# A fused attention and feed-forward kernel: the dilated heads' v loads issued from ScalarE's queue

## Chip, cores and metric

One NeuronCore of a Trainium2 chip runs the whole kernel. The metric is device time of one execution in microseconds (us); lower is better.

## What is computed

Attention over q, k and v of shape (4 batches, 8 heads, 576 positions, 64), then two feed-forward layers on the 2304 x 512 result. All in float32; the weights come as float64.

```
mask_plain = (rel >= 0) & (rel < window)                                   # heads 0 to 3, window 32
mask_dil = (rel >= 0) & (rel < window * dilation) & (rel % dilation == 0)  # heads 4 to 7, dilation 4
scores = where(mask, scale * q @ k.T, -1e9)
attn = exp(scores - max); attn = attn / (sum(attn) + 1e-9)
x = (attn @ v) as [2304 tokens, 512]
x = (silu(x @ w_gate) * (x @ w_val)) @ w_out                               # d_ff 1536
out = (((x @ w1) * (x @ w2)) @ w3) @ w_out2                                # d_ff 1024
```

## The kernel before

**Stages.** Attention runs first, in 18 superblocks of 128 tokens, software-pipelined: step u of the loop (L531, u from -3 to 19) works on several superblocks at once. Then TensorE does the feed-forward layers in 20 slices of 128 hidden units by 5 groups of tokens (L472 up, L565 and L585 down, L612 the product w3 @ w_out2). Each float32 product is three matmuls of high and low parts.

**Loads of attention.** `load_qk(u)` (L292) brings a superblock's q and k into `near` (heads 0 to 3, L297) and `far` (the dilated heads, L302). `load_v(u)` (L305) brings v into `vnear` (L314, two blocks of up to 96 rows) and `vfar` (L319, 96 rows of the dilated heads). A `far` or `vfar` window that crosses a multiple of 144 rows, the length of one dilated stream, is cut into two loads, so the 18 superblocks have 27 `vfar` loads. All of these, and the weights' loads (`raw_w`, L143 and L148), are issued from the SP queue, in the order of the program: it holds no list or planner of its own, and an instruction waits for all before it on its queue. Buffers: three of `near` and of `far`, four of `vnear` and of `vfar`; a load waits until the last reader of its buffer is done.

**One step u** (`attention_step`, L495, then `attention_end`, L522) issues in this order: loads of q and k for superblock u+5; loads of v for u+2; on ScalarE the copies of the transposed probabilities out of PSUM (`t_p_out`, L417, u-1) and of the attention result (`x_out_hi`, L451, u-2); exp on ScalarE (L389, u+1); scores on TensorE (L368, u+2), on VectorE mask and maximum (L377, L383), on GpSimd the subtraction (L384); the transposes of q and k on TensorE (`pnear` L341, `pfar` L348, u+3), with copies on ScalarE (L335, L336 for the 32 keys kept from the superblock before, then L343, L344, L349, L350); a piece of weight conversion on VectorE (L114 to L124); the sums and reciprocals on VectorE (L393 to L396, u+1) and the normalisation on GpSimd (L402); the low part of the attention result on VectorE (L455, u-2). At its end TensorE transposes the probabilities of u (L411) and multiplies those of u-1 with v (`av`, L431).

So the v of superblock u+2, called for in step u, is read at the end of step u+3, and the `vfar` buffer that it takes was last read by av of u-2, at the end of step u-1; `x_out_hi(u-2)` on ScalarE reads the result of that same av.

Of the kernel before, what the change touches and what calls it, by code (L numbers as in the profile page):

```python
# [19 lines left out]
P = 128  # L20
WINDOW = 32
DIL = 4
QB = 64
KW = QB + WINDOW
NIDLE = 8
NEG = -1.0e9
# bounds of a float64's upper word (sign off, read as float32) between which float32 has its exponent
UP_LO = 2.0 ** -15
UP_HI = 2.0 ** 16 * (1.0 + (2 ** 23 - 2 ** 20 - 1) / 2.0 ** 23)

# [2 lines left out]
def attention_ffn_kernel(  # L33
# [14 lines left out]
    nc = tc.nc  # L48
# [10 lines left out]
    RES = S // DIL  # L59
# [12 lines left out]
    wp = ctx.enter_context(tc.tile_pool(name="wp", bufs=1))  # L72
    sp = ctx.enter_context(tc.tile_pool(name="sp", bufs=1))
    ps = ctx.enter_context(tc.tile_pool(name="ps", bufs=1, space=PSUM))
    # tokens in two parts: what attention still writes is apart from what the first groups read
    CUT = groups[(len(groups) + 1) // 2][0]
    spans = ((0, CUT), (CUT, NT))
    x_hi = [xp.tile([P, KT, b - a], F32R, name=f"x_hi{a}") for a, b in spans]
# [3 lines left out]
        i = int(t0 >= CUT)  # L82
        return x[i][:, kk, t0 - spans[i][0]:t0 - spans[i][0] + n]

    # keep the tensor engine busy until the first loads are there: its clock is halved when it comes from idling
    zeros = xp.tile([P, 512], BF16, name="zeros")
    nc.vector.memset(zeros, 0.0)
    idle = ps.tile([P, 512], F32, tag="po3", name="idle", bufs=1)
# [7 lines left out]
        return ps.tile([P, 512], F32, tag=tag, name=name, bufs=bufs)  # L96


    # ---------------------------------------------------------------- weights
    WC = 2 * KT * P + DM  # L100
    PW = KT * P
    NCH = NFT + NF2
# [4 lines left out]
        return w.bitcast(I32)  # L107

    def to_f32(dst, raw):
        """float64 words (low, high) of raw -> float32 bits in dst, one instruction at a time."""  # L110
        w = raw.rearrange("p (n t) -> p n t", t=2)
        up, low = w[:, :, 1], w[:, :, 0]
        b = dst.bitcast(I32)
        nc.vector.tensor_scalar(out=b, in0=up, scalar1=0x7FFFFFFF, scalar2=None, op0=ALU.bitwise_and)  # L114
        yield
        nc.vector.tensor_scalar(out=dst, in0=dst, scalar1=UP_LO, scalar2=UP_HI, op0=ALU.max, op1=ALU.min)
        yield
        nc.vector.tensor_scalar(out=b, in0=b, scalar1=3, scalar2=0x3FFFFFFF,
                                op0=ALU.logical_shift_left, op1=ALU.bitwise_and)
        yield  # L120
        nc.vector.scalar_tensor_tensor(out=b, in0=up, scalar=-0x40000000, in1=b,
                                       op0=ALU.bitwise_and, op1=ALU.bitwise_or)
        yield
        nc.vector.scalar_tensor_tensor(out=b, in0=low, scalar=29, in1=b,  # L124
                                       op0=ALU.logical_shift_right, op1=ALU.bitwise_or)
        yield
# [7 lines left out]
                      wp.tile([P, WC], F32R, tag="wlo", name=f"wlo{c}", bufs=2))  # L134
        return whl[c]

    # a job is one [P, PW] piece of float64 weights, loaded ahead and brought to float32 in order
    def job_load(job):
        kind, a, j = job
        raw = wp.tile([P, 2 * PW], I32, tag="wraw", name=f"raw_{kind}{a}_{j}", bufs=3)  # L140
# [30 lines left out]
    jobs = []  # L171

    def jobs_of(c):
        """Jobs of the steps of slice c: by group."""
        res = [[] for _ in groups]
        if c + 1 < NCH:
            first = 1
            if NFT - 1 <= c:
                f = c + 1 - NFT
                res[0].append(("w3", f, 0))  # L180
                res[1].append(("w3", f, 1))
                first = 2
            for j in range(3 if c + 1 < NFT else 2):
                res[first + j].append(("w", c + 1, j))
        if 1 <= c <= NJ:
            res[4].append(("wo", c - 1, 0))
        return res
# [19 lines left out]
    running = run_jobs()  # L207

    def next_job():
        """The rest of a job."""  # L210
        while not next(running):
            pass

# [1 line left out]
    parts = [0]  # L215

    def part_jobs(u):
        """The early jobs, an instruction or two at a time over the superblocks."""
        n = len(early)
        if u >= -2 and (u + 2) % (NU // n - 2) == 0:  # L220
            load_to(min(n, jpos[0] + 1))
        upto = min(PARTS, max(0, (u - 1) * PARTS // (NU - 5)))
        while parts[0] < upto:
            next(running)
            parts[0] += 1

    # ---------------------------------------------------------------- attention
    att = tc.alloc_tile_pool(name="att", bufs=1, side="right")

    # Superblock u, blocks of QB queries with KW keys each:  # L230
    # - first half of the heads: tokens u*P.. of all batches
    # - second half of the heads: indices u*QB.. of the streams (batch, pair of residues), each of RES
    #   indices
    # index of a stream's first query in a superblock (from the superblock's start)
    starts = {}
    for part in range(NU * QB // RES):
        for u in range(NU):
# [7 lines left out]
    def build_masks():  # L245
        gen = att.tile([P, KW], F32, name="m_gen")
        nc.gpsimd.memset(gen, 0.0)
        for h in range(2):
            g = gen[h * QB:(h + 1) * QB, :]
            # row - col + WINDOW >= 0, and col - row - 1 >= 0  # L250
            nc.gpsimd.affine_select(out=g, in_=g, compare_op=ALU.is_ge, fill=NEG,
                                    base=WINDOW, pattern=[[-1, KW]], channel_multiplier=1)
            nc.gpsimd.affine_select(out=g, in_=g, compare_op=ALU.is_ge, fill=NEG,
                                    base=-1, pattern=[[1, KW]], channel_multiplier=-1)
        for u in range(MPER):
            m = att.tile([P, 2, KW], F32, name=f"mask{u}")
            nc.vector.tensor_copy(out=m, in_=gen.rearrange("p (u c) -> p u c", u=1).to_broadcast([P, 2, KW]))
            for h in range(2):
                g = m[h * QB:(h + 1) * QB]
                if (2 * u + h) % NB == 0:  # L260
                    nc.gpsimd.memset(g[:, 0, 0:WINDOW], NEG)
                if u in starts:
                    d = starts[u]
                    if d <= 0:
                        nc.gpsimd.memset(g[:, 1, 0:WINDOW + d], NEG)
                    else:
                        # rows from d on see none of the keys before d
                        w = g[:, 1, 0:WINDOW + d]
                        nc.gpsimd.affine_select(out=w, in_=w, compare_op=ALU.is_ge, fill=NEG, base=d - 1,
                                                pattern=[[0, WINDOW + d]], channel_multiplier=-1)  # L270
            mask.append(m)

    def runs(a, n, size):
        """Rows a..a+n cut at multiples of size: (row, length, index of the part, offset in it)."""
        done = 0
        while done < n:
            part, off = divmod(a + done, size)
            step = min(n - done, size - off)
            yield done, step, part, off
            done += step  # L280
# [4 lines left out]
    near_in, far_in, v_in = {}, {}, {}  # L285

    def stream(src, part):
        """Rows [RES, HH, 2 * D] of a stream: both residues of an index side by side."""
        b, r = divmod(part, RP)
        return src[b, HH:H].rearrange("h (m r) d -> m h (r d)", r=DIL)[:, :, r * 2 * D:(r + 1) * 2 * D]  # L290

# [13 lines left out]
    def load_v(u):  # L305
# [10 lines left out]
        if z:  # L316
            nc.gpsimd.memset(far[0:z], 0.0)
        for row, cnt, part, m in runs(u * QB - WINDOW + z, KW - z, RES):
            nc.sync.dma_start(out=far[z + row:z + row + cnt], in_=stream(v, part)[m:m + cnt])  # L319
        v_in[u] = near, far  # L320

    qkT = {}

    def t_qk(u):
        """Transposed queries (scaled) and keys: partitions are (head's parity, d), or (residue, d)."""
        qn = att.tile([P, HP, P], F32, tag="qn", name=f"qn{u}", bufs=3)
        qf = att.tile([P, HH, QB], F32, tag="qf", name=f"qf{u}", bufs=3)
        kn = att.tile([P, HP, WINDOW + P], F32, tag="kn", name=f"kn{u}", bufs=3)
# [23 lines left out]

    sc, sm, mx, rs, pt_, pT, avp = {}, {}, {}, {}, {}, {}, {}

    # Row tile rt of the scores, half x of its queries: first half of the heads: head 2p+rt, block x;
    # second half: head 2p+x, residue rt.
    def scores(u, rt):
        t = bank("pa", f"sc{u}_{rt}", 2)[:, :NP * KW].rearrange("q (p c) -> q p c", c=KW)
        qn, qf, kn, kf = qkT[u]
# [73 lines left out]
        avp[u] = t  # L433

    def x_parts(x, u):
        """(columns of x, columns of av's result) of superblock u."""
        t = avp[u]
        yield tokens(x, slice(0, HP), u * P, P), t[:, 0:HP, :]
        t = t[:, HP:NP, :].rearrange("d p (h q) -> d p h q", h=2)
# [9 lines left out]
    def x_out_hi(u):  # L449
        for dst, src in x_parts(x_hi, u):  # L450
            nc.scalar.copy(out=dst, in_=src)  # L451
# [3 lines left out]
            nc.vector.tensor_tensor(out=dst, in0=src, in1=hi.bitcast(F32), op=ALU.subtract)  # L455
        avp.pop(u)

    # ---------------------------------------------------------------- feed-forward, slice of hidden units by slice
    st = {}

    upp = {}
# [27 lines left out]
        nc.gpsimd.tensor_tensor(out=sl[:, :n], in0=pr[:, :n], in1=sh[:, :n].bitcast(F32), op=ALU.subtract)  # L489
        st[c, g] = sh, sl  # L490

    # ---------------------------------------------------------------- attention, software-pipelined
    build_masks()

    def attention_step(u):  # L495
        def live(n):
            return 0 <= n < NU
        if live(u + 5):
            load_qk(u + 5)
        if live(u + 2):  # L500
            load_v(u + 2)
        if live(u - 1):
            t_p_out(u - 1)
        if live(u - 2):
            x_out_hi(u - 2)
        if live(u + 1):
            softmax_e(u + 1)
        if live(u + 2):
# [42 lines left out]
            nc.vector.tensor_tensor(out=dst, in0=src, in1=dst, op=ALU.add)  # L551

    def down1(c, g):
        """y of the first layer: channels on partitions."""
        t0, n = groups[g]
        hi, lo = whl[c]
        sh, sl = st.pop((c, g))
# [12 lines left out]
                nc.gpsimd.tensor_tensor(out=xl, in0=y[:, cc, :], in1=xh.bitcast(F32), op=ALU.subtract)  # L570

    def down2(c, g):
        """Output rows: tokens on partitions."""
        t0, n = groups[g]
        hi, lo = whl[c]
        sh, sl = st.pop((c, g))
# [13 lines left out]
    def down(c, g):  # L590
        (down1 if c < NFT else down2)(c, g)

    # ---------------------------------------------------------------- w3 @ w_out2, a row tile ahead of its slice
    w3T = {}

    def fold_t(f, half):
# [66 lines left out]
```

## Time and profile before

| What | Value |
|---|---|
| Time before, median of 3 runs (lowest to highest) | 906.69 us (905.39 to 908.28) |
| Span of the profiled execution (its own time is not listed apart) | 905.6 us |
| TensorE busy | 885.6 us (98%) |
| VectorE busy | 603.3 us (67%) |
| ScalarE busy | 245.2 us (27%) |
| GpSimd busy | 286.5 us (32%) |
| Loads from the SP queue | 60.90 MB |

The profile is one execution, recorded by the hardware. "Busy" counts an engine's instructions, not its waits or its issues of DMAs; SP does nothing but issue and wait, so it is read from its timeline. PE is TensorE, PEld its weight loads, DVE VectorE, ACT ScalarE, POOL GpSimd; an engine's name with a q is its queue. The shares are means over two stages that differ: attention, about the first 103 us, and the feed-forward layers after it. A load has two times: how long its queue took to issue it, and how long from its issue to its landing.

### The profile page before, as it was taken

The numbers are of one execution on the slowest core, as the hardware profiler recorded it, in microseconds if no ns is written. First come the engines' busy times: TensorE is split into PE (matmuls) and PEld (weight loads), VectorE is DVE, ScalarE is ACT, GpSimd is POOL, SyncE is SP. The second block draws the span as 40 slices with busy tenths as digits, with TensorE's granted clock in tenths as the row PEclk, the third lists the DMA queues.
The fourth block names the chain that finished last, engine by engine and source line by source line (L and its number), as shares of the span: only waits on it lengthen the run. The fifth ranks groups of instructions, "written<-read, shape, count | busy, mean of one in ns | idle before, by whom it ended". The sixth has DMA issues, their size and how long they took to land.

```text
span 905.6 us, 13322 instructions
## 1 busy us (share of the span) xinstructions
PE 885.6 (98%) x5256; PEld 744.7 (82%) x5256; DVE 603.3 (67%) x1070; ACT 245.2 (27%) x510; POOL 286.5 (32%) x280
## 2 busy tenths in 40 slices
PE   7898999999999999999999999999999999999998
PEld 4777888888888888888888888888888888888886
DVE  6789755767567676676674687857575747575724
ACT  5777621222122222122212133212121212121211
POOL 6566612323233232232322257321221212121211
PEclk9999999999999999999999999999999999999999
DMA  6896601122112121121210211112020211120014
GB/s 164 187 193 155 171 25 47 47 70 70 48 47 71 47 70 46 47 70 47 70 47 26 67 47 47 47 47 67 27 70 25 70 46 48 47 66 28 1 47 163
DMA packets 79118, 61.75 MB, mean 68 GB/s; under 512 B 35664, under 2 KB 72144, under 8 KB 79056
## 3 DMA queue, kind: packets, MB, share of 16 engines
q1 hardware_dynamic: 79056, 60.90, 23.8%
q8 instruction: 42, 0.69, 0.3%
q14 instruction: 20, 0.16, 0.1%
HBM read 56.16 MB, written 4.72 MB: 67 GB/s over the span
## 4 chain that ended last, share of the span: by engine, by line
PE 90%; DMA 4%; DVE 3%; SPq 1%; ACT 1%; issue 0%; POOL 0%; DVEq 0%; POOLq 0%
PE pa L472 27%; PE pb L472 26%; PE po L565 15%; PE po L585 10%; PE fold L612 5%; DMA far<-in_k_dram 4%; PE av L431 2%; PE pp L411 1%; PE pfar L348 1%; PE sc L368 1%; SPq L302 1%; PE pw L600 1%; DVE o L551 0%; PE pnear L341 0%; ACT x_hi L569 0%
## 5 line engine op out<-in xcount | busy, mean ns | idle before, releaser
L489 POOL TENSOR_TENSOR sl<-pr,sh 128x512 fp32r<-128x512 f32 (+1 forms) x100 | 118.2, 1182 | 332.9 <-ACT sh L488 332.9
L485 DVE TENSOR_TENSOR pr<-pb,ga 128x512 f32<-128x512 f32 (+1 forms) x100 | 63.8, 638 | 223.2 <-PE pb L472 147.5
L472 PE MATMUL pa<-x_hi,whi 128*128 128x512 f32 (+1 forms) x400 | 149.0, 372 | 0.0
L472 PE MATMUL pa<-x_hi,wlo 128*128 128x512 f32 (+1 forms) x400 | 147.6, 369 | 0.0
L472 PE MATMUL pa<-x_lo,whi 128*128 128x512 f32 (+1 forms) x400 | 147.5, 369 | 0.0
L472 PE MATMUL pb<-x_hi,wlo 128*128 128x512 f32 (+1 forms) x400 | 147.1, 368 | 0.0
L472 PE MATMUL pb<-x_hi,whi 128*128 128x512 f32 (+1 forms) x400 | 147.1, 368 | 0.0
L472 PE MATMUL pb<-x_lo,whi 128*128 128x512 f32 (+1 forms) x400 | 147.1, 368 | 0.0
L169 POOL TENSOR_TENSOR wlo<-val_w,whi 128x512 fp32r<-128x512 f32 x52 | 67.0, 1289 | 206.9 <-ACT whi L168 206.8
L551 DVE TENSOR_TENSOR y<-po,y 128x512 f32<-128x512 f32 (+1 forms) x220 | 131.5, 632 | 0.0
L488 ACT CAST sh<-pr 128x512 fp32r<-128x512 f32 (+1 forms) x100 | 57.9, 579 | 187.1 <-DVE pr L485 187.1
L168 ACT CAST whi<-val_w 128x512 fp32r<-128x512 f32 x52 | 32.3, 622 | 225.9 <-DVE val_w L124 225.9
L565 PE MATMUL po<-sl,whi 128*128 128x512 f32 (+1 forms) x240 | 88.5, 369 | 0.6 <-POOL sl L489 0.6
L565 PE MATMUL po<-sh,whi 128*128 128x512 f32 (+1 forms) x240 | 88.5, 369 | 0.0
L565 PE MATMUL po<-sh,wlo 128*128 128x512 f32 (+1 forms) x240 | 88.3, 368 | 0.0
L472 PEld LDWEIGHTS pa<-x_hi,wlo 128*128 128x128 f32 x400 | 75.3, 188 | 12.9
L472 PEld LDWEIGHTS pa<-x_lo,whi 128*128 128x128 f32 x400 | 75.5, 189 | 12.7
L472 PEld LDWEIGHTS pa<-x_hi,whi 128*128 128x128 f32 x400 | 75.4, 189 | 12.7
L472 PEld LDWEIGHTS pb<-x_lo,whi 128*128 128x128 f32 x400 | 75.4, 189 | 12.5
L472 PEld LDWEIGHTS pb<-x_hi,wlo 128*128 128x128 f32 x400 | 75.4, 189 | 12.5
L472 PEld LDWEIGHTS pb<-x_hi,whi 128*128 128x128 f32 x400 | 75.4, 189 | 12.4
L551 DVE TENSOR_TENSOR o<-po,o 128x512 f32<-128x512 f32 x126 | 83.8, 687 | 0.2 <-PE po L585 0.2
(92 smaller groups left out, 1360.3 us busy)
## 6 DMA issues: line engine op xcount, KB each, us to landing
raw_w<-in_moe_w_dram SPq DMA_DIRECT2D x32, 512.0 KB, 3.6
raw_w<-in_moe_w_gate_dram SPq DMA_DIRECT2D x12, 512.0 KB, 3.5
raw_w<-in_moe_w_val_dram SPq DMA_DIRECT2D x12, 512.0 KB, 3.6
raw_w<-in_moe_w_out_dram SPq DMA_DIRECT2D x12, 512.0 KB, 3.5
out_dram<-o SPq DMA_DIRECT2D x18, 256.0 KB, 2.1
raw_wo<-in_moe_w_out_dram SPq DMA_DIRECT2D x8, 512.0 KB, 3.4
vnear<-in_v_dram SPq DMA_DIRECT2D x32, 96.0 KB, 3.9
near<-in_q_dram SPq DMA_DIRECT2D x16, 128.0 KB, 3.5
```

Of the source, the lines that this page charges most:

```text
L168: nc.scalar.copy(out=hi, in_=val)
L169: nc.gpsimd.tensor_tensor(out=lo, in0=val, in1=hi.bitcast(F32), op=ALU.subtract)
L302: nc.sync.dma_start(out=far[r0:r0 + cnt], in_=stream(src, part)[m:m + cnt])
L431: nc.tensor.matmul(out=t[o * D:(o + 1) * D, p, c * QB:(c + 1) * QB], lhsT=lhsT, rhs=pp[:, p, x * QB:(x + 1) * QB], start=True, stop=True)
L472: nc.tensor.matmul(out=pt[:, :n], lhsT=a[:, ws], rhs=tokens(x, kk, t0, n), start=first and kk == 0, stop=last and kk == KT - 1)
L485: nc.vector.tensor_tensor(out=pr[:, :n], in0=pb[:, :n], in1=ga[:, :n], op=ALU.mult)
L488: nc.scalar.copy(out=sh[:, :n], in_=pr[:, :n])
L489: nc.gpsimd.tensor_tensor(out=sl[:, :n], in0=pr[:, :n], in1=sh[:, :n].bitcast(F32), op=ALU.subtract)
L551: nc.vector.tensor_tensor(out=dst, in0=src, in1=dst, op=ALU.add)
L565: nc.tensor.matmul(out=po[:, :n], lhsT=a[:, ws], rhs=x[:, :n], start=first, stop=last)
L585: nc.tensor.matmul(out=po, lhsT=x[:, ts], rhs=a[:, ws], start=first, stop=last)
L612: nc.tensor.matmul(out=pt, lhsT=a[:, j % HJ, :], rhs=b[:, j, :], start=first and j == 0, stop=last and j == NJ - 1)
```

## The change

`vfar`'s loads are issued from ScalarE's queue, and in a step `load_v` is called after the two kinds of copies on ScalarE rather than before them. Elsewhere the diff takes out comments, which are left out here.

```diff
         for row, cnt, part, m in runs(u * QB - WINDOW + z, KW - z, RES):
-            nc.sync.dma_start(out=far[z + row:z + row + cnt], in_=stream(v, part)[m:m + cnt])
+            nc.scalar.dma_start(out=far[z + row:z + row + cnt], in_=stream(v, part)[m:m + cnt])
         v_in[u] = near, far
...
         if live(u + 5):
             load_qk(u + 5)
-        if live(u + 2):
-            load_v(u + 2)
         if live(u - 1):
             t_p_out(u - 1)
         if live(u - 2):
             x_out_hi(u - 2)
+        if live(u + 2):
+            load_v(u + 2)
         if live(u + 1):
             softmax_e(u + 1)
```

## Rows read from the trace of the kernel before

**Rows 1.** Chain in order of time, 0 to 120 us: start, length, what.

```profile
2.54 3.30 DMA far<-in_k_dram
...
40.54 5.07 DMA far<-in_k_dram
...
102.99 2.96 PE pa L472 x12
```

**Rows 2.** Timeline of SP, 0 to 115 us: start, length, engine, line, operation, tiles.

```profile
0.75 0.44 SPq L297 DMA_DIRECT2D near<-in_q_dram  x1
...
12.63 1.73 SPq L319 DMA_DIRECT2D vfar<-in_v_dram  x1
...
19.83 0.95 SPq L314 DMA_DIRECT2D vnear<-in_v_dram  x2
20.83 0.48 SPq L319 DMA_DIRECT2D vfar<-in_v_dram  x1
21.40 0.42 SPq L297 DMA_DIRECT2D near<-in_q_dram  x1
...
102.37 0.45 SPq L148 DMA_DIRECT2D raw_w<-in_moe_w_out_dram  x1
```

**Rows 3.** Instructions of the load lines: count, ns min/median/max; landing.

```profile
L302 SPq DMA_DIRECT2D far<-in_q_dram x24: 417/607/1392, 1.8 to 91.2; - x24
L314 SPq DMA_DIRECT2D vnear<-in_v_dram x36: 330/482/1776, 11.3 to 100.2; - x36
L319 SPq DMA_DIRECT2D vfar<-in_v_dram x27: 312/457/1736, 12.6 to 100.8; - x27
DMA to landing us min/median/max: 2.3/3.8/5.0
```

**Rows 4.** Timeline of VectorE, 0 to 100 us: what ended its idle time.

```profile
26.93 0.56 DVE L377 TENSOR_TENSOR s<-sc,mask 128x384 f32<-128x384 f32 x1 [5.54 <-PE sc L368]
...
36.66 0.56 DVE L377 TENSOR_TENSOR s<-sc,mask 128x384 f32<-128x384 f32 x1 [0.33 <-PE sc L368]
...
50.87 0.56 DVE L377 TENSOR_TENSOR s<-sc,mask 128x384 f32<-128x384 f32 x1 [3.33 <-PE sc L368]
...
78.27 0.56 DVE L377 TENSOR_TENSOR s<-sc,mask 128x384 f32<-128x384 f32 x1 [1.41 <-PE sc L368]
...
93.99 0.56 DVE L377 TENSOR_TENSOR s<-sc,mask 128x384 f32<-128x384 f32 x1 [0.43 <-PE sc L368]
```

**Rows 5.** Busy time by engine, 8 to 52 and 52 to 103 us, and sum.

```profile
core 0: us, PE busy (x) PEld busy (x) DVE busy (x) ACT busy (x) POOL busy (x), PEclk, DMA share, GB/s
8.00:52.00 44.00, 36.60 (x543) 30.57 (x539) 33.12 (x70) 28.99 (x81) 25.34 (x31) 0.92 0.85 184
52.00:103.00 51.00, 45.35 (x756) 39.03 (x753) 47.74 (x101) 38.73 (x107) 36.83 (x43) 1.00 0.78 172
sum 95.00, PE 81.95 PEld 69.60 DVE 80.86 ACT 67.71 POOL 62.16; mean PE 40.98 PEld 34.80 DVE 40.43 ACT 33.86 POOL 31.08
```

**Rows 6.** Timeline of TensorE, 17 to 50 us: transposes of q and k.

```profile
19.43 0.41 PE L341 MATMUL pnear<-ident,near 128*128 128x128 f32 x2 [1.48 <-DMA near<-in_q_dram]
21.78 1.09 PE L348 MATMUL pfar<-ident,far 128*128 128x128 f32 x4 [1.25 <-DMA far<-in_k_dram]
...
45.74 1.08 PE L348 MATMUL pfar<-ident,far 128*128 128x128 f32 x4 [0.73 <-DMA far<-in_k_dram]
```

**Rows 7.** The same table, 20 to 25 and 45 to 50 us.

```profile
20.00:25.00 5.00, 3.63 (x23) 3.03 (x25) 1.32 (x3) 2.26 (x6) 2.74 (x4) 0.66 0.80 188
45.00:50.00 5.00, 4.27 (x47) 3.79 (x47) 2.47 (x6) 2.46 (x6) 2.69 (x3) 0.66 1.16 206
```

**Rows 8.** Waits of the SP queue, 7 to 103 us: total, times, longest.

```profile
SPq L297 <- DMA near<-in_q_dram: 0.5, 1, 0.5
```

**Rows 9.** Timeline of ScalarE, 26 to 32 us.

```profile
26.11 0.92 ACT L451 CAST x_hi<-av 128x256 fp32r<-128x256 f32 x2 [0.92 <-PE av L431]
...
30.84 0.94 ACT L451 CAST x_hi<-av 128x256 fp32r<-128x256 f32 x2 [0.74 <-PE av L431]
```

## The prediction

> **What bounds the kernel now.** I read the chain of waits in order of time first, then the queue and the engines that it names, each by its timeline. From 102.99 us on the chain is TensorE's feed-forward matmuls to the end; before that, in the attention stage, it comes back again and again to one kind of piece, the landing of a superblock's dilated keys, `far<-in_k_dram` [rows 1]. So the change, which touches loads of the attention stage alone, can move the start of the feed-forward part, and each microsecond won there should come off the total.
>
> Why are those keys late? SP's timeline answers: from 0.75 us to 102.82 us (102.37 plus 0.45) it issues 157 loads nearly without a pause; the rows around 20 us follow each other with gaps of 0.05 to 0.10 us [rows 2]. That is 102.07 / 157 = 0.65 us per load, long issues and waits included. SP is a queue that never catches up, and the keys stand in it behind everything else, the 27 `vfar` loads too.
>
> How much of that is lost time? TensorE's idle time is the wrong measure, because VectorE has its own work to do meanwhile. VectorE's timeline shows five idle stretches that end with a wait for scores: 5.54, 0.33, 3.33, 1.41 and 0.43 us, 11.04 us together [rows 4]. Between them it works without a break: from 52 to 103 us it is busy 47.74 of 51 us [rows 5]. Faster loads can take away those 11.04 us and no more; behind them stands VectorE.
>
> **The change, part by part.** *SP loses 27 issues.* At the mean of 0.65 us each, the loads behind them come earlier. By the count of mask pairs on VectorE, the gap of 5.54 us belongs to superblock 4 and that of 3.33 us to superblock 8. Ahead of superblock 8's keys, the queue holds the dilated v loads of superblocks 0 to 4: 1, 1, 2, 1 and 2 pieces (a window of 96 rows cut at multiples of 144), seven in all. 7 x 0.65 = 4.6 us, less than the 5.54 + 0.33 + 3.33 = 9.2 us of idle up to there, so 4.6 us is what the queue gives by then. Ahead of superblock 13's keys (gap 1.41 us) it is 15 pieces, 9.8 us, more than the 4.6 + 1.41 + 0.43 = 6.4 us that could be used; those two gaps close whole. Sum: 6.4 us.
>
> Bounds of this term: with the median issue of `vfar`, 0.457 us [rows 3], it is 7 x 0.457 + 1.84 = 5.0 us. At the other end all 11.0 us go: the `vfar` issue at 12.63 us took 1.73 us, and if such long ones leave SP with the loads they hit, seven pieces are worth more than seven means. I take the mean, because long issues hit every load line (up to 1.39, 1.78 and 1.74 us in [rows 3]) and so seem to come with the queue, not with `vfar`.
>
> *The clock* is inside these gaps. Four transposes of `far` took 1.09 us at 21.78 us and 1.08 us at 45.74 us [rows 6], in stretches whose granted clock averaged 0.66 [rows 7], a mix of 2.4 and 1.2 GHz; at 21.78 us TensorE had just idled 1.48 and 1.25 us for loads. If the idling shrinks enough, some of this goes too; I count nothing for it, and the upper bound of 11.0 us holds it.
>
> *ScalarE gains 27 issues.* The trace has no load on this engine, so I price one by SP's: 0.457 us median for `vfar`, 0.31 to 1.74 us at the ends [rows 3]. 27 x 0.457 = 12.3 us. ScalarE is busy 67.7 of the 95 us from 8 to 103 us [rows 5]; with 12.3 it is 80.0, just under VectorE's 80.9. I cost it at nothing, and the cover is ScalarE's own waiting: at 30.84 us it had idled 0.74 us for av before its x_hi copy [rows 9], more than one median issue per superblock. Behind a load on ScalarE stand that superblock's exp, the copies of the key halos and the four copies out of `pnear` and `pfar`; VectorE's sums wait for exp, TensorE's next scores for the copies. If the cover goes, the second rival below happens.
>
> *Waits.* A `vfar` load must wait until av has read its buffer four superblocks back. ScalarE has passed that wait already: the x_hi copy just before it reads the same av. SP also waits for landings of older loads that the new load does not read (0.5 us once [rows 8]), since the program hands its loads a few completion counters in turn. On ScalarE such a wait can stand too. With eight counters, the load waited for was issued about 8 x 0.65 = 5.2 us before and lands after 3.8 us, at most 5.0 for `vfar` [rows 3], so I take nothing; the highest is a part of the second rival.
>
> *The new place in the step.* The call moves past pT and x_hi copies, which issue only on ScalarE. The near v loads stay on SP and the zeroing on GpSimd, both in their old order; no cost. The v rows themselves are wanted by av three steps later, some 15 us against 3.8 us of landing, so a `vfar` that starts late makes nothing late.
>
> **Sum.** 6.4 us off the profiled span of 905.6 us gives 899.2; the median of the runs is 1.1 us above that span, so I forecast 906.7 - 6.4 = 900.3 us. A difference under 0.3%, 2.7 us, could not be told from none.
>
> **Rival 1: the keys land no earlier.** Then it is not the issue that limits but what comes after it, or the two queues take turns and SP is held while ScalarE issues. For it: from 45 to 50 us the DMA share is 1.16 at 206 GB/s [rows 7], so transfers already overlap, and one `vfar` lands after 2.3 us in the best case and 5.0 in the worst [rows 3]. Against it: over the whole first part the share is 0.85 [rows 5], and issue to issue SP has no gap to wait in. The same bytes would then arrive at the same pace, the five gaps would stay, and the time would be 906.7 us, no change.
>
> The Trainium skill's page "DMA: Bandwidth & Descriptors", section "Issuing engines are not separate DMA queues", speaks for this rival: several issuing engines share the same 16 DMA engines and save only issue time, usually small beside the transfer. By that rule alone the sum would be near 0; the trace agrees that an issue is short beside a landing (0.457 against 3.8 us), but also shows issues back to back. "Perfetto Trace Analysis", section "DMA Instruction — HWDGE (DVE, Sync)", adds that the generator of descriptors is locked by one issuer at a time; no run here shows that yet.
>
> **Rival 2: ScalarE becomes the bound, slower.** Place: the load between x_hi and exp, in every superblock. Price: 67.7 + 27x us must fit into the 95 us of the stage. It decides at x = (95 - 67.7) / 27 = 1.01 us for which one load holds ScalarE, issue and wait together; from 1.11 us on the loss shows. At 1.40 us, about what a long issue of `far` takes [rows 3], it is 105.5 us, 10.5 more than now: 917 us. Against it: the medians, 0.46 to 0.61 us. For it: nothing bounds a wait for a landing, and ScalarE would wait in order.
>
> A third way, that the change does not do what it says, I leave out: `vfar` has this one issue line.
>
> **How the numbers follow.** Forecast 0.60: SP without a pause and the keys in the chain are strong signs. Rival 1 0.21, rival 2 0.19. These are the chances of faster, same and slower as well. The range runs from 895.5 us (all 11.0 us won) through rival 1 up to 911 us, rival 2 with x = 1.17 us (67.7 + 31.6 = 99.3, 4.3 more than 95). What rival 2 leaves above that, and a gain beyond VectorE's gaps, I put at under 2 in 10 together. The forecast's own range, with the bounds of its term, is 895.5 to 901.7 us.
>
> **What would show it.** Right: SP's issues of `far` keys earlier by about 4 us at superblock 8; VectorE's waits for scores in the attention stage down from 11.0 to about 4 or 5 us; the first feed-forward matmul near 96.6 us instead of 102.99; one `vfar` issue on ScalarE near 0.5 us. Rival 1: the same gaps on VectorE, landings longer, or issues on either queue longer while the other issues. Rival 2: idle stretches on VectorE and TensorE that end with exp or with ScalarE's copies, and `vfar` issues or waits of over 1 us on ScalarE. The forecast is wrong if the first feed-forward matmul starts at or after 102.99 us.

## The result and the profile after

The changed kernel is slower: 913.14 us median of 10 runs (908.76 to 918.55) against 908.09 us (905.39 to 910.32, 10 runs) on the same chip, a ratio of 1.0057 with a 95% interval of 1.0041 to 1.0073. That is some 5 us more where 6.4 us less was forecast, and 2 us above the top of the range. Executions of one kernel spread over several us here, so a profile, which is one execution, is read for what happens in it, and the ratios for how much.

| | before | after |
|---|---|---|
| median, us | 908.09 | 913.14 |
| profiled execution, us (span) | 906.7 (905.6) | 910.98 (909.2) |
| first feed-forward matmul, us | 102.99 | 106.49 |
| VectorE busy / ScalarE busy, from 8 us to there | 80.86 / 67.71 | 80.75 / 68.81 |

The chain of waits in order of time (start, length, what), to hold against [rows 1]:

```profile
12.75 8.19 DMA raw_w<-in_moe_w_gate_dram
21.34 2.71 DMA far<-in_k_dram
...
38.01 0.01 ACT x_hi L451
38.02 4.87 DMA vfar<-in_v_dram
42.89 0.02 issue
42.90 4.42 DMA far<-in_k_dram
...
60.54 5.99 DMA vfar<-in_v_dram
66.54 2.64 DMA far<-in_k_dram
...
96.58 0.38 ACTq L319
96.96 0.34 ACT x_hi L451
97.30 0.12 ACTq L319
97.42 1.17 issue
98.59 0.84 ACT s L389
...
106.49 2.99 PE pa L472 x12
```

The landing of `vfar`, which no piece of the chain before is in this stage, now stands on it, directly ahead of dilated keys, twice. At 38.01 us av lets ScalarE copy x_hi; behind that copy ScalarE issues a `vfar`; when that has landed, at 42.89 us, SP issues the keys of superblock 8, 0.01 us later. Before, SP issued those keys at 40.54 us [rows 1]. The keys do not read `vfar`. SP stands there because the program hands a few completion counters to its loads in turn, whichever of the two queues issues them, and a load waits until the one that last used its counter has landed. The instructions' operands in the trace bear this out: the loads of SP carry eight counters, those of ScalarE are out of the same eight, and each of the five loads or waits of SP counted below names the counter of the `vfar` that it waits for.

The waits of SP's queue (engine and line, what it waited for: total us, times, longest), in the stretch up to 112 us, with a load as the releaser:

```profile
SPq L314 <- DMA vfar<-in_v_dram: 5.4, 3, 2.6
...
SPq L302 <- DMA vfar<-in_v_dram: 3.6, 2, 3.2
SPq L302 <- DMA raw_w<-in_moe_w_gate_dram: 2.3, 1, 2.3
```

9.0 us in five waits for a `vfar` to land, where SP waited for no `vfar` before. SP's timeline around the longest of them (start, length, engine, line, operation, tiles):

```profile
62.76 0.60 SPq L302 DMA_DIRECT2D far<-in_q_dram  x1
66.54 0.60 SPq L302 DMA_DIRECT2D far<-in_k_dram  x1
```

From 63.36 to 66.54 us, 3.18 us, SP issues nothing, with its next load ready to go; ScalarE had issued the `vfar` at 60.54 us. VectorE's idle stretches (the number in brackets), to hold against [rows 4]:

```profile
11.27 0.56 DVE L377 TENSOR_TENSOR s<-sc,mask 128x384 f32<-128x384 f32 x1 [0.53 <-PE sc L368]
...
29.67 0.56 DVE L377 TENSOR_TENSOR s<-sc,mask 128x384 f32<-128x384 f32 x1 [7.72 <-PE sc L368]
...
45.71 0.56 DVE L377 TENSOR_TENSOR s<-sc,mask 128x384 f32<-128x384 f32 x1 [0.94 <-PE sc L368]
51.30 0.56 DVE L377 TENSOR_TENSOR s<-sc,mask 128x384 f32<-128x384 f32 x1 [0.66 <-PE sc L368]
80.21 0.56 DVE L377 TENSOR_TENSOR s<-sc,mask 128x384 f32<-128x384 f32 x1 [2.71 <-PE sc L368]
97.33 0.56 DVE L377 TENSOR_TENSOR s<-sc,mask 128x384 f32<-128x384 f32 x1 [1.98 <-PE sc L368]
```

From 12 us on the five stretches of before, 11.04 us, are five again, of 14.01 us. The first grew by 2.2 us: ScalarE, which no longer has SP's queue in front of it, issued the first five `vfar` pieces between 7.84 and 18.59 us, where SP had come to them between 12.63 and 31.33 us. They run beside superblock 4's q and k, which are wanted sooner. What came in the middle shrank (3.66 to 1.60 us), what came late grew (1.84 to 4.69 us).

The granted clock of TensorE takes part too. Behind the last of these gaps the chain has the same three pieces in both kernels, first before, then after, each followed by the row of the busy table for 90 to 95 us (columns as in [rows 5], the clock is the first number behind POOL's):

```profile
90.15 0.63 PE pfar L348 x4
90.78 0.87 PE pp L411 x8
91.66 1.48 PE av L431 x32
90.00:95.00 5.00, 4.77 (x80) 4.19 (x80) 4.43 (x11) 3.86 (x13) 3.48 (x4) 1.00 0.75 185
```

```profile
91.94 0.85 PE pfar L348 x4
92.79 1.71 PE pp L411 x8
94.50 2.00 PE av L431 x32
90.00:95.00 5.00, 3.91 (x21) 3.07 (x22) 4.86 (x13) 3.37 (x9) 3.77 (x5) 0.72 0.99 212
```

They take 4.56 us where they took 2.98: 1.58 of the 3.5 us by which the feed-forward part starts later. TensorE had just idled 0.47, 0.19 and 0.64 us for loads, and the clock of 0.72 is a mix of 2.4 and 1.2 GHz. The kernel before had a stretch like this at 45 us [rows 7], with more work of the stage still behind it.

ScalarE is not the bound: from the end of that av to the first feed-forward matmul it is 9.99 us (96.50 to 106.49), and 9.85 before (93.14 to 102.99), though two of its loads stand on the chain there. Its loads, from the instructions of the load line (count, ns min/median/max), to hold against [rows 3], and the busy time from 8 us on (columns as in [rows 5]):

```profile
L319 ACTq DMA_DIRECT2D vfar<-in_v_dram x27: 318/376/1542, 7.8 to 101.2; - x27
```

```profile
8.00:106.50 98.50, 82.13 (x1313) 70.71 (x1313) 80.75 (x172) 68.81 (x189) 62.30 (x75) 0.95 0.81 179
```

### The profile page after: what moved, and what is told of

The parts are those of the page before. It is cut to its first block, busy times and chain, and to the rows that moved or that the text cites. A ratio compares the mean times of both kernels' runs of the same rounds, so it can differ in the third digit from the quotient of the medians.

```text
span 909.2 us, 13310 instructions
## 1 busy us (share of the span) xinstructions
PE 886.3 (97%) x5256; PEld 746.0 (82%) x5256; DVE 602.5 (66%) x1070; ACT 246.0 (27%) x510; POOL 286.8 (32%) x280
## 4 chain that ended last, share of the span: by engine, by line
PE 90%; DMA 4%; DVE 2%; SPq 1%; ACT 1%; issue 1%; POOL 0%; ACTq 0%; DVEq 0%
PE pa L472 27%; PE pb L472 26%; PE po L565 15%; PE po L585 10%; PE fold L612 5%; PE av L431 2%; DMA far<-in_k_dram 2%; PE pp L411 2%; DMA vfar<-in_v_dram 1%; DMA raw_w<-in_moe_w_gate_dram 1%; PE sc L368 1%; PE pfar L348 1%; PE pw L600 1%; SPq L302 1%; DVE o L551 0%
## 5 line engine op out<-in xcount | busy, mean ns | idle before, releaser
L169 POOL TENSOR_TENSOR wlo<-val_w,whi 128x512 fp32r<-128x512 f32 x52 | 67.2, 1292 | 208.7 <-ACT whi L168 208.7
```

The lines of the kernel that those rows point to most:

```text
L169: nc.gpsimd.tensor_tensor(out=lo, in0=val, in1=hi.bitcast(F32), op=ALU.subtract)
```

## Experiments

Two theories were set up from these views, and a third beside them. **A**: the early `vfar` loads, in front of superblock 4's q and k. **B**: the shared completion counters, through which SP's q and k wait for a `vfar` that ScalarE issues late. **C**: SP's issue was never the limit, since the DMA engines were full. Each kernel was run in five rounds against the kernel before on the same chip; the chip is not the same for all, so kernels are compared by these ratios. The table gathers the runs; the last three columns are read from one profiled execution each (SP's waits for a `vfar` to land; SP's issue of the last dilated keys; the first feed-forward matmul in TensorE's timeline, 0.07 us ahead of the chain's piece). Those of end_place and v_later_scalar took 912.74 and 913.46 us, 2 to 3 us more than the medians of their kernels, 910.91 and 910.16.

| kernel | ratio to before (95%) | waits for vfar, us (times) | last keys issued, us | feed-forward, us |
|---|---|---|---|---|
| before | 1 | 0 | 91.84 | 102.92 |
| after | 1.0057 (1.0041 to 1.0073) | 9.0 (5) | 92.28 | 106.42 |
| late_scalar | 1.0033 (1.0019 to 1.0048) | 5.4 (3) | 91.39 | 104.81 |
| early_scalar | 1.0006 (0.9992 to 1.0020) | 1.1 (1) | 90.34 | 102.98 |
| gpsimd_all | 1.0044 (1.0030 to 1.0058) | 0 | 83.82 | 106.55 |
| gpsimd_late | 1.0039 (1.0025 to 1.0053) | 0 | 88.03 | 105.50 |
| no_vfar | 0.9962 (0.9947 to 0.9977) | 0 | 80.41 | 100.19 |
| quarter_vfar | 0.9983 (0.9968 to 0.9998) | 0 | 89.48 | 101.33 |
| quarter_scalar | 0.9992 (0.9975 to 1.0009) | 6.3 (6) | 88.80 | 102.82 |
| old_place | 1.0091 (1.0071 to 1.0110) | 14.4 (10) | 96.51 | 111.31 |
| end_place | 1.0027 (1.0012 to 1.0042) | 17.8 (10) | 95.71 | 108.19 |
| v_later | 0.9968 (0.9953 to 0.9983) | 0 | 87.25 | 99.35 |
| v_later_scalar | 1.0022 (1.0005 to 1.0039) | 15.0 (8) | 96.16 | 108.89 |
| v_raw_later | 1.0007 (0.9989 to 1.0025) | 0 | 89.51 | 102.98 |

**Late or early alone.** One edit each, at the `vfar` load of the changed kernel:

```
-            nc.scalar.dma_start(out=far[...], ...)
+            (nc.sync if u < 4 else nc.scalar).dma_start(out=far[...], ...)    late_scalar
+            (nc.scalar if u < 4 else nc.sync).dma_start(out=far[...], ...)    early_scalar
```

> The vfar loads of superblocks 0 to 3 are back on SP, those from superblock 4 on stay on ScalarE. Theory A (early loads): ScalarE issues the first five vfar pieces at 7.84 to 18.59 us, ahead of superblock 4's q and k, and these land 2.7 us later (24.30 against 21.65 us); put back, the time is that of the kernel before or better (ratio 0.995 to 1.001), and VectorE's first gap returns from 7.7 to about 5.5 us. Theory B (completion counters): from 30 us on SP still stands until a vfar that ScalarE issued late has landed (2.63 us at 33.67, 3.18 us at 66.54, 1.84 us at 84.89), so most of the loss of 5.1 us stays (ratio 1.003 to 1.006).

> Only the vfar loads of superblocks 0 to 3 go out on ScalarE, all later ones on SP. Theory A: the loss stays, ratio 1.002 to 1.006, with a first gap of VectorE near 7.7 us. Theory B: SP stands behind a vfar at most once or twice, before 35 us, and the ratio is 0.998 to 1.002.

With the later superblocks alone on ScalarE the loss stays, 1.0033; with the first four alone it is 1.0006, which can't be told from none. So B's half of the loads carries the larger part (of late_scalar's 5.4 us of waits, 0.7 are for a `vfar` of SP itself). A's mechanism is there all the same and is worth less than it looks: in early_scalar VectorE's first gap is 7.8 us, as long as in the changed kernel, but the gaps behind it shrink.

```profile
29.20 0.56 DVE L377 TENSOR_TENSOR s<-sc,mask 128x384 f32<-128x384 f32 x1 [7.81 <-PE sc L368]
...
76.64 0.56 DVE L377 TENSOR_TENSOR s<-sc,mask 128x384 f32<-128x384 f32 x1 [1.57 <-PE sc L368]
...
92.53 0.56 DVE L377 TENSOR_TENSOR s<-sc,mask 128x384 f32<-128x384 f32 x1 [0.45 <-PE sc L368]
```

A gap that comes early gives SP time to run ahead, and part of it comes back. late_scalar also shows the counters holding the other queue. Here is ScalarE's timeline:

```profile
25.80 0.65 ACT L451 CAST x_hi<-av 128x256 fp32r<-128x256 f32 x1
30.03 1.40 ACTq L319 DMA_DIRECT2D vfar<-in_v_dram  x2
31.47 0.84 ACT L389 ACTIVATE s<-s 128x768 f32<-128x768 f32 x1 [5.03 <-DMA far<-in_q_dram]
```

ScalarE stands behind x_hi until 30.03 us: its `vfar` names the counter of a `near` load of SP that landed at 30.01 us and that it doesn't read. The two issues take 1.40 us more, so exp stands behind x_hi for 5.03 us (its row names the load of SP whose counter the second `vfar` took over); VectorE's sum then waits 3.47 us for exp.

**Counters apart: GpSimd as the issuer.** Loads issued on GpSimd have completion counters of their own, and SP's instructions are the same, in the same order, as in the changed kernel (gpsimd_all):

```
-            nc.scalar.dma_start(out=far[...], ...)
+            nc.gpsimd.dma_start(out=far[...], ...)                              gpsimd_all
+            (nc.sync if u < 4 else nc.gpsimd).dma_start(out=far[...], ...)    gpsimd_late
```

> All vfar loads are issued on GpSimd, whose loads have completion counters of their own, so no load of SP waits for a vfar to land. Theory B: with those waits (9.0 us in all) gone the gain that was forecast shows, 2 to 6 us faster than before, ratio 0.993 to 0.998, unless GpSimd's own work (subtractions 31.9 and products 29.0 us in all) is held up by issuing. Theory A: the first five vfar pieces still go out early, and superblock 4's q and k land late, so the ratio is 1.002 or more.

> vfar of superblocks 0 to 3 on SP, later ones on GpSimd: neither early loads in front of superblock 4's q and k nor shared completion counters. If A and B together are the whole story, the forecast's gain remains: 2 to 6 us faster than before, ratio 0.993 to 0.998. A third theory, C: SP's issue never was the limit, since 6 to 7 loads are in flight and the 16 DMA engines set the pace; then the ratio is 0.998 to 1.002 even here.

By the ratios both expectations of B missed: both kernels are slower than before. The loss that A expected of gpsimd_all came, but gpsimd_late, with no early load, lost as much. By the trace the half that concerns SP came true. No load of SP waits for a `vfar`, and SP issues its last dilated keys at 83.82 us:

```profile
83.82 0.62 SPq L302 DMA_DIRECT2D far<-in_k_dram  x1
```

That is 8.0 us earlier than before (91.84) and 8.5 us earlier than with ScalarE as the issuer (92.28), though there, too, SP had lost 27 issues. These keys landed at 88.80 us, against 95.02 before. So a second queue does free SP, once its loads don't share counters with SP's, and C in its plain form falls: the keys can come earlier. Something of C is left: from issue to landing a `far` load takes 4.5 us in the median here, 3.3 before. What ate the gain is VectorE, busy 88.79 us up to the feed-forward part instead of 80.86:

```profile
8.00:106.60 98.60, 84.40 (x1307) 70.56 (x1297) 88.79 (x173) 68.56 (x187) 78.83 (x101) 0.95 0.94 187
```

The groups of VectorE's instructions that grew, in gpsimd_all (8 to 103 us: busy, mean ns of one | idle before); before, the first took 5.4 us at 319 ns, the second 1.8 at 589, the third 2.6 at 854:

```profile
L394 DVE TENSOR_SCALAR mx<-mx 128x8 f32<-128x8 f32 x16 | 8.3, 517 | 0.5
L116 DVE TENSOR_SCALAR val_w<-val_w 128x512 f32<-128x512 f32 x3 | 4.1, 1380 | 0.0
L124 DVE SCALAR_TENSOR_TENSOR val_w<-raw_w,val_w 128x512 int32<-128x512 int32 x3 | 4.0, 1343 | 0.0
```

2.9 + 2.3 + 1.4 = 6.6 of the 7.9 us more. In gpsimd_all twelve instructions of these three groups ran at least 1.3 times as long as the shortest of their group, all of them beside tensor work of GpSimd (L384, L169); before it was six. The timelines of GpSimd and VectorE in gpsimd_late show one case. GpSimd's issues push its subtraction on by 1.19 us, into a weight conversion of VectorE that starts at the same time and takes 2.15 us:

```profile
45.07 1.19 POOL L319 DMA_DIRECT2D vfar<-in_v_dram  x2
46.26 1.62 POOL L384 TENSOR_TENSOR s<-s,mx 128x384 f32<-128x384 f32 x2
```

```profile
46.29 2.15 DVE L124 SCALAR_TENSOR_TENSOR val_w<-raw_w,val_w 128x512 int32<-128x512 int32 x1
```

The Trainium skill's page "SBUF — State Buffer", section "SBUF: two separate sides", says that VectorE, in some modes or with two inputs in SBUF, and GpSimd take one pair of ports in turn, each for a whole instruction; the trace agrees as far as it goes, with 2.15 against a mean of 0.85 us.

**What the loads cost where they were.** From the kernel before, with all loads on SP: no_vfar leaves out the 22 `vfar` loads from superblock 4 on, and quarter_vfar issues them with one head of four. In both, av reads older rows in place of what isn't loaded.

```
no_vfar       +            if u < 4:
                               nc.sync.dma_start(out=far[...], ...)
quarter_vfar  +            few = slice(0, HH if u < 4 else 1)
              +            nc.sync.dma_start(out=far[..., few], in_=...[..., few])
```

> The kernel before, without the 22 vfar loads of superblocks 4 to 17: av reads the tiles of superblocks 0 to 3 in their place, so part of the output is computed from other v rows. It takes away the issue on SP and the bytes too, with no load on another queue. The forecast said that 0.65 us of SP per vfar makes the keys late: by it the attention stage loses up to 5.5 us of waits for scores (all but superblock 4's gap), ratio 0.993 to 0.996. If the vfar loads cost the stage nothing even where they are, the ratio is 0.998 to 1.002, and the term of the forecast was empty from the start.

> The kernel before, with all 27 vfar loads issued on SP, but those of superblocks 4 to 17 bring one head of four (a quarter of the bytes; the rest of the tile is stale, so part of the output is computed from other v rows). If SP's issue is what counts, this gains nothing or little (ratio 0.998 to 1.002) where no_vfar gains. If the bytes on the DMA engines count (theory C), it gains three quarters or more of what no_vfar gains.

Without the loads the time falls by 0.38%, 3.4 us; with the issues kept and three quarters of the bytes gone, by 0.17%, 1.5 us. So the forecast's term was not empty, but some of it may lie in the bytes, which the change doesn't remove: three quarters of them bring 0.17 of 0.38. The intervals are too wide for more: 0.9983 also lies in the range that was set for issues alone, and 0.9962 just above the range for no_vfar.

**A light load on ScalarE's queue.** quarter_scalar is quarter_vfar with the light loads moved, at the changed kernel's place in the step:

```
+            (nc.sync if u < 4 else nc.scalar).dma_start(out=far[..., few], in_=...[..., few])
```

> quarter_vfar with its light vfar loads of superblocks 4 to 17 (one head of four, the rest of the tile stale) moved to ScalarE's queue, at the changed kernel's place in the step; the first four superblocks stay on SP. Theory B (completion counters): the bytes no longer matter, the late issue does, so SP still stands until a light vfar has landed, and the move costs again: 2 to 4 us more than quarter_vfar (0.9983), ratio 1.000 to 1.003. Theory C (the DMA engines were full, and one more queue only crowds them): with a quarter of the bytes there is room, and the move costs nothing or gains, ratio 0.994 to 0.998.

0.9992 against 0.9983, with intervals that overlap: neither theory's numbers. SP still waits 6.3 us for `vfar`, in six waits of 1.05 us on average, against 1.8 in the changed kernel. What the move costs here is not resolved: by the two intervals it lies between a gain of 0.14% and a loss of 0.32%. That a light load lets SP go sooner fits, but is not shown.

**The place in the step.** Three places for the load on ScalarE, all other loads untouched: ahead of the pT and x_hi copies (old_place), behind them (the changed kernel), and behind exp and the q and k copies (end_place).

```
         if live(u + 5):
             load_qk(u + 5)
+        if live(u + 2):          old_place
+            load_v(u + 2)
...
             x_out_hi(u - 2)
-        if live(u + 2):
-            load_v(u + 2)
...
             t_qk(u + 3)
+        if live(u + 2):          end_place
+            load_v(u + 2)
```

> The changed kernel with the load call at its old place in the step, so ScalarE issues vfar ahead of the pT and x_hi copies and not behind them; the queue is still ScalarE's. Theory B (completion counters): vfar goes out a few us earlier in each step, SP waits less for it to land (less than the 9.0 us of the changed kernel), and the ratio to before is 1.001 to 1.005; but ScalarE now waits itself for the read of the old buffer by av, ahead of copies that others need. If the place makes no difference the ratio stays at 1.004 to 1.007.

> The changed kernel with the vfar loads (still on ScalarE, with the vnear loads on SP called beside them) at a third place: behind exp and the query and key copies of the step, ahead of the weight work. Theory B in numbers: in the runs so far SP's waits for a vfar to land and the loss go together (9.0 us and 0.57% at the changed kernel's place, 14.4 us and 0.91% at the old place, 5.4 us and 0.33% with superblocks 4 and later alone), about 0.06% of loss per us waited. Further down the step a load's turn in the rotation comes later too, and exp is no longer behind it; I expect 3 to 8 us of such waits and a ratio of 1.002 to 1.005, in that proportion. If the ratio goes its own way while the waits stay under 3 us, something other than these waits makes the loss (the crowded DMA engines, or ScalarE being held by the issue).

The direction was wrong for old_place: further ahead in the step SP waits more, 14.4 us, and it is the slowest kernel of all, 1.0091. It is here that ScalarE itself is held, at the load: its waits up to 111 us show it idle 19.5 + 4.6 us ahead of the pT copies that now stand behind the load, where the changed kernel has 1.7 us ahead of them and 7.8 us ahead of x_hi. old_place has 6 runs, the other kernels 9 or more.

```profile
ACT pT L417 <- PE sc L368: 19.5, 9, 4.3
...
ACT pT L417 <- PE av L431: 4.6, 3, 2.1
```

So behind x_hi, which waits for the same read of the old buffer, was the better place of the two, as the prediction had it. For end_place the expected size was wrong: 17.8 us of waits, more than anywhere, and yet only 1.0027 (the profiled execution by itself 912.74 us, 1.0050 of the median before). So the sum of SP's waits tells where the coupling is, not what it costs; the proportion of 0.06% per us that I had taken from three kernels doesn't hold. That a wait costs only what is late behind it, and that SP makes up some of it, fits but is argued.

**The order on one queue.** v_later keeps all loads on SP and issues a superblock's v loads one step later, behind the q and k that are wanted sooner; v_later_scalar moves its `vfar` to ScalarE; v_raw_later is v_later with the three early weight loads two steps later.

```
-        if live(u + 2):
-            load_v(u + 2)
+        if live(u + 1):
+            load_v(u + 1)                                             v_later
...
-            nc.sync.dma_start(out=far[...], ...)
+            nc.scalar.dma_start(out=far[...], ...)                    v_later_scalar, behind x_out_hi
...
-        if u >= -2 and (u + 2) % (NU // n - 2) == 0:
+        if u >= 0 and u % (NU // n - 2) == 0:                         v_raw_later
```

> The kernel before, all loads on SP, but the v loads of a superblock (vnear and vfar) are issued one step later, so superblock 4's q and k stand in the queue ahead of v(0) and v(1) and so on. Theory A says that the order at the start sets the gap of 5.54 us before superblock 4: three loads fewer ahead of its keys, at 0.65 us, give 2.0 us, and the ratio is 0.996 to 0.999. If the DMA engines have room and the order does not matter, 0.999 to 1.001. The risk is av: its v rows then have some 10 us from issue to use, against 3.5 to 4.1 us of landing.

> v_later with all vfar loads moved to ScalarE's queue, behind its pT and x_hi copies as in the changed kernel. With v one step later no vfar goes out ahead of superblock 4's q and k at the start, so theory A costs nothing here. Theory B: SP waits 5 us or more for vfar landings, and the move costs v_later its gain: ratio 0.999 to 1.005 against 0.9968 without the move. If A was the larger part of the loss, the ratio stays at 0.995 to 0.998.

> v_later, all loads on SP, and the three early weight loads raw_w two steps later each. In v_later the first raw_w, issued at 11.30 us, lands 6.50 us later and holds back superblock 4's q and k behind it; with it out of the way the remaining gaps before superblocks 4 and 5 (2.31 and 3.20 us) shrink by 1 to 3 us: ratio 0.993 to 0.997. If the gaps only move to the next superblock, 0.997 to 0.998.

v_later is faster than both kernels, 0.9968, 905.38 us against 907.97, with the whole computation in place. VectorE's waits for scores from 20 us on, in its timeline:

```profile
24.09 0.56 DVE L377 TENSOR_TENSOR s<-sc,mask 128x384 f32<-128x384 f32 x1 [2.31 <-PE sc L368]
31.95 0.56 DVE L377 TENSOR_TENSOR s<-sc,mask 128x384 f32<-128x384 f32 x1 [3.20 <-PE sc L368]
79.78 0.56 DVE L377 TENSOR_TENSOR s<-sc,mask 128x384 f32<-128x384 f32 x1 [0.87 <-PE sc L368]
```

6.38 us, against 11.04 before: the gap of 5.54 us is split in two (2.31 and 3.20) rather than closed, and it is the later ones that go. The same move of `vfar` to ScalarE turns this 0.9968 into 1.0022, 0.54% between them, about what it costs in the change itself. Two `vfar` pieces still go out ahead of superblock 4's q and k, at 9.81 and 11.98 us, which its expectation had ruled out, so A is not excluded here. But the first gap, 5.52 us, is as long as v_later's two together (5.51), and the loss comes later: gaps of 2.49, 0.18, 4.09 and 3.43 us from 50 us on, where v_later has 0.87. v_raw_later failed: the weight conversion waited on VectorE itself (2.90 us for `raw_w` at 28.51 us), and a gap of 3.93 us came back at 83.53 us; 1.0007 can't be told from no change.

**The clock over the runs.** Within one kernel the time goes with the granted clock of the execution: the ten runs of the changed kernel go from 908.76 us at a mean of 0.994 to 918.55 us at 0.981. Their mean is 0.990, that of the 106 runs of the kernel before in these experiments 0.994; the latter took 907.7 us on average at 0.994 and 910.0 from 0.989 to 0.991. A line through those 106 gives 0.47 us per 0.001. By that estimate some 1.8 us of the 5 us lost go with the lower clock and some 3.3 us are lost at equal clock; of v_later's gain of 2.5 us in the mean, 1.7 go with a higher one (0.997 against 0.993). Whether the waits for loads bring the clock down, or it only happens to differ, no run separates.

## Why the prediction was wrong, step by step

**What bounds the kernel: right.** The feed-forward part starts later by 3.5 us in the profiled execution, whose span is 3.6 us longer. no_vfar and v_later, which bring the keys earlier, start it 2.7 and 3.6 us earlier and are faster, though no_vfar's profiled span is only 0.8 us shorter.

**SP loses 27 issues, 0.65 us each: the issues were saved, but no gain arrived.** The forecast priced issues alone. no_vfar can be priced by the same working: two of the seven pieces ahead of superblock 8 are gone, 2 x 0.65 = 1.3, plus the 1.84 us behind, 3.1 us; measured were 3.4 us. That they agree is no test of issues alone, since no_vfar takes the bytes away too, and gpsimd_all gives less: its 21 fewer loads ahead of the last keys brought them 8.0 us earlier, 0.38 us each. With ScalarE as the issuer SP spent 67.1 us issuing ahead of its last keys, where it had spent 80.8, and yet reached them at 92.28 us, not earlier than 91.84: the 13.7 us saved were given back standing, 9.0 of them for a `vfar` to land. The forecast's own range has a slip: 906.7 less the 11.0 us of all gaps is 895.7, not 895.5 us.

**Waits: the step that failed.** The prediction said that a counter's former load was "issued about 8 x 0.65 = 5.2 us before and lands after 3.8 us", "so I take nothing". That sum holds for one queue that issues in its own order without a pause. I asked only whether ScalarE would wait for SP, and not the reverse: with two queues in one rotation, SP's load waits for a `vfar` that ScalarE issued late, because it stood behind x_hi and so behind av: 2.8 us before in the longest wait here, and in old_place, end_place and v_later_scalar once each only after SP had begun to wait. In the changed kernel SP waited 9.0 us in five such waits. The next step's sentence "a `vfar` that starts late makes nothing late" was true of av, which reads the rows, and false of SP, which borrows the counter.

**ScalarE costed at nothing: nearly right, though it gained more issue time than priced.** One load took 376 ns in the median, not 457, but the long ones bring the 27 to 14.9 us in all (0.55 us each), not 12.3; ScalarE's busy time, which doesn't count issues, hardly moved (67.71 to 68.81 us). Two loads stand on the chain at 96.58 and 97.30 us, close ahead of the feed-forward part, with 1.17 us behind the second before exp starts; yet this last stretch is only 0.14 us longer than before. Rival 2 had the sign for a reason that is only a small part, and its break-even of 1.01 us per load was not reached.

**The clock, counted at nothing as a gain that might come on top: it went the other way.** In the profiled execution it cost 1.58 us behind the last gap, and over the runs it was lower than before (0.990 against 0.994).

**The start of the stage: missed.** I counted what SP loses and not that ScalarE would come to the first `vfar` pieces sooner, in front of superblock 4's q and k. The first gap grew from 5.54 to 7.72 us where I had expected it to shrink. early_scalar shows that this alone costs little.

**Rival 1: right about the gain, silent about the loss.** It rested in part on the Trainium skill's page "DMA: Bandwidth & Descriptors", section "Issuing engines are not separate DMA queues", which lets several issuers save issue time alone. By that rule the change would have cost nothing; it lost 0.57%. The other page of the Trainium skill that the prediction named there, "Perfetto Trace Analysis", section "DMA Instruction — HWDGE (DVE, Sync)", on its locked generator, finds no support in the medians: a `far` q load took SP 607 ns before [rows 3] and 602 after. The means leave it open: SP's 12 `far` issues that ran while ScalarE issued took 802 ns, the 36 others 540, but a long issue is also likelier to meet one of the other queue.

**What stays open.** late_scalar shows that the move of the later `vfar` loads costs 0.33%, v_later_scalar that the move costs 0.54% in another order, and the chain shows SP's keys released by a `vfar` that landed. How the loss divides between SP's waits, ScalarE's own (5.03 us once in late_scalar), the clock and the bytes of two queues side by side is not settled: the waits and the ratios are not in proportion, and quarter_scalar lies between the theories. A ScalarE queue with counters of its own was not tried.

## What to carry to other kernels

Before moving a load to another engine's queue, ask what ties the two queues together: if their loads share completion counters in turn, a busy queue can inherit the delays of the engine that it was meant to be free of, and the chain shows it as a load released by the landing of one that it doesn't read. An engine that issues in between its own work was a poor place here for a load whose counter a tight queue needed next. Where one queue is full, look first at its order: putting the loads that are wanted later behind those that are wanted sooner won 0.32% here, with no load on another queue.

## What was unexpected of the hardware

- One load's landing varies by a factor of two with what runs beside it: the first weight load `raw_w` landed 4.3 us after its issue before, and 8.19 us in the changed kernel, where ScalarE's `vfar` pieces run beside it; the other kernels with such early pieces have 7.0 to 8.7 us. v_later has 6.5 us without any, so they are not the only cause.
- Issuing a load on GpSimd is not free for VectorE: 27 of them, 642 ns each on GpSimd, made VectorE 7.9 us busier, through instructions of GpSimd that slid into VectorE's.
